# A scan step in two VectorE operations instead of three, gate products in pairs, and a new order of the first stage

## The chip, the cores and the metric

The kernel runs on one core of a Trainium2 chip. The metric is the time of one execution on the device in microseconds; runs are compared by their median. Five engines take part: TensorE (PE in the profile, its weight loads PEld), VectorE (DVE), ScalarE (ACT), GpSimd (POOL) and the queue that issues all transfers (SP).

## The reference, cut to what matters

Three blocks follow each other. The first is an attention with a complex state: 4 batches and 8 heads, 768 positions, head dimension 48. The second is a gated layer (384 to 1536 to 384), the third another one (384 to 2048 to 384), both on 3072 tokens.

```
for t in range(S):
    new_re = ar * S_re - ai * S_im          # ar, ai of position t, |a| held under 0.999
    new_im = ar * S_im + ai * S_re
    S_re, S_im = new_re + outer(k[t], v[t]), new_im
    y[t] = q[t] @ S_re
x = rms_norm(y) * rms_g
u = silu(x @ w_gate) * (x @ w_val)          # 384 -> 1536, "gate product"
h = (u @ w_out) @ w_in2
out = (h * clip(h + 3, 0, 6) / 6) @ w_out2
```

## The kernel before, in words

The recurrence is done in chunks. Seven units of positions (`UNITS`, line 21), the first and the last of 32 positions per chunk, the five between of 64, with two chunks (`c`) side by side in the partitions. In a unit the products of the factors `a` are formed by a scan over half a chunk: `step` (line 443) multiplies the running complex product in `P` by the next factor. It is written three times per position: one product `m4` of 2x2x48 elements (line 449: imaginary and real factor times real and imaginary product), one sum for the new imaginary half (line 451), one difference for the new real half (line 452). `LAt` holds the normalised factors of one unit in two planes, imaginary then real; `steps_norm` (f1 to f8, line 378) makes them, f7 the imaginary plane and f8 the real one. There are 16 such positions in the first and in the last unit and 32 in each of the others, 192 in all.

After the scan of unit n its factors give scaled keys and queries (`sq`, `k1`, `k2`, `x2`, `x1`), which TensorE transposes (`tr`), multiplies into scores (`scores`), chunk sums (`sums`) and outputs (`outs`). `emit_F` (line 554) makes the factors that carry the state from chunk to chunk, of 16 elements per operation, once for each group `g` of batches. `state` updates the carried state, `flip` transposes the normalised output into `x`. Keys, swapped halves of the state and gate products travel through DRAM (`kwrite`, `kload`, `swap`, `u_dr`).

The gated layer follows per half unit of 256 tokens (`steps_M`, line 748). For each of 12 column groups j (`J1`) there are six `gemm` steps: w = 0 the gate and w = 1 the value, three parts of the inner dimension each, and each `gemm` is three matmuls (`mm3`, lines 744 to 746) because a number is kept as a high and a low part. Gate and value of one j share a tile of PSUM, `pm`, 2 x 256 columns; four such tiles rotate. `silu(j)` then applies Silu on ACT to the gate half (line 766), multiplies by the value half on DVE (line 768) and, at odd j, sends both into `u_dr`.

The first stage has its order written out by hand. `ORDER` (line 34) names, two characters each, which step goes on by one part next, and each engine gets its instructions in exactly that order; a part that must wait holds everything behind it on its engine. `ON_POOL` lists the steps whose products (`ttx`, line 364) run on GpSimd instead of VectorE: 16 of them. Behind the written order come the last unit's gated layer and the later layers (line 996 on), which the change leaves as they are except that `silu` is shared.

Of the kernel before, what the change touches and what calls it, by code (L numbers as in the profile page):

```python
# [9 lines left out]
F32 = mybir.dt.float32  # L10
# [8 lines left out]
XW = 112  # L19
IM = 64  # L20
# [26 lines left out]
    "90837z837A84afa290ah7z7Ea97Cag84a97E85857Cai86aj7F91ar7Ban7Faqar7Barao8-aoarak86aoal7P8-am87ap87as88as888989ap938a7Qas7Qapawas93ax7Rayataz7SaAaB7XaD7TaEaFaC7VaG"
    "7UaHaJaIaKaLaCaJ7WaM8aaN8baJaO8baPanaR8c8daS8danaT8eaU8eaV8caWaYaZaQ8fa+aX8faQa-aXb0b1b28g8gaXb3b4b2b58hb68c8hb78ib88iba8jbb8jbc8kbd8wbebfb9bh8xbibgb9bjbkbnbgbl"
    "8xb9bmbobnbpbq8ybnbrbQaubQ8kau8m8zbQbu8l8mbT8naubs8AdlbtbvbwdkbxaubybubB8BbzbAav8nbC8l8FbD8obE8obR8pbIbR8pbF8qbGbRbH8qbJ8rbK8r8lbL8sbM8sbN8tbObBdC8tccdD8udEbPbB"
    "dF8vbIdG8CdH8DdJdK8vdL8DdM8HdN8EbWdIbS8GdPdObWdQdRbPdSdIdPbPdT8vdUbSbSdPdVdXbSdY8IdZ8Jd+d-8Je0e28Ke3e48Me58LdWe6e7e18NbScde9bSbZbSdWeadsebece8edceeebZbXefdob+bX"  # L50
    "doegehb+bUeidobYbVc0cee1e8ejdseke1elendseoepefeqbYercfesefc0eudmcfdoc1dnb-c1dpcgb-evdqchc2dsdremetc2c3cjewdtduemeAc3c4etc5etc4duexeyc5duezeBeCcickeDeEdueFeGeIcu"
    "eJcueKeHcvdvcveOdvcwcwcxcxdvcyeLcyeMczeNdveAc9eHc6eOc9czeHdwclePc6eQc8cAdycAc8dycBcBcCcCdAcDdyc7cDcbcEc7dycbeReSeWcEeVdzeWcacFcFeYcaeWeZeXeZeXdxeZeTeUeXclf2eZf3"
    "cGf4cGf5cHf6cHf7dxdBcIcme+f8cIe+cmcJcJcnf9e+faeVcKfbfce+dBctfdeVfecofge-fhffcqfifjcrfkflcpfnfocLfpcKf8csfqfmfffmfrftfsfff0ftcLf0gpcMcMftcNcNgmf0hTcOfucOfvgmfwf0"
    "hSfxgmfyfAcPfzf1cPfBcQfCfDcQfEcRfFcRfHfGcSfIcSfJcUcTfKcUfLcVfMcVfOfNcWfPcWfHfQcXfOcKfRfScTfTfAgncXcYfUfHfWcTcYd2fXfYgncZfZcZf+c+f-c+g1fVd3g2g3g4g0fVg5g7d8gng6fV"
    "g0g8c-d3g9gagKgbc-gcd0gdd4gfd1ggghgegigjglg7gkgei8dbd9i9d5d1iaibd9icg7ddgodaidd6d1ifigihiiijikglimded7iniogodfglipiedfiqilieirilitdgiuiviliwdcdhixiydiiAiBisiCiz"
    "djgogLiDgoiEiFiHgogoiIiJiKgohWiGiLisiNiMiziGgxiziNgsgMgxiNiOiPgsh+gqiQiRgriSiTgMiVhWiWiXiYh+iZi+hWgtj0h+gthUgNhWhVgwgviUgNj1hXgwiUgOhYgvgPi-guhZgyh+gugyj2gQj3gz"
    "j6i0gzj4h-i0gRgSgAi0j5j7h0j8gAgBi0gCh0h1i1gCh1h2i1h2h3h3i1j9h4jah4jbjdh5jci1gBjejfjgi-h5i2gHh6i-h6gDh7gHh7i4gDh8i4h8h9h9gJhai6i4hagEgJhbgTjhgEjigGjkhbhcgFi4gGj6"
    "gFjjjdjlhcjmjdjvi5gIjvgIjsjsjnjojvjpjri3jshdgTi3juhdhejvjtjqhei7hfjthfgUjwhgjwjtgUjkjAhgjrjBi7jwjrjCjDjEjFjHgVhgjIjJgWjKg-jLjwjMjOgZjPgXjQjGjRjSjxjGgYjTjNjVjUjW"
# [12 lines left out]
ON_POOL = {34, 132, 138, 171, 570, 814, 840, 862, 1104, 1140, 1146, 1150, 1388, 1396, 1614, 1715}
# [164 lines left out]
def attn_moe(tc, io, dbg=None):  # L236
# [64 lines left out]
    LAt = ap.tile([128, 2 * 32 * D], F32, name="LAt", tag="LAt")  # L301
# [40 lines left out]
    def lav(u):  # L342
        n = UNITS[u][0] // 2 * D
        return LAt[:, 0:2 * n].rearrange("p (x n) -> p x n", x=2)

    def steps_load(u):
        C, _ = UNITS[u]
        n = C // 2 * D
        o = _acol(u)

        def f():
            if C == 64 and UNITS[u - 1][0] == 32:
                nc.gpsimd.memset(P[:, 17:33, D:IM], 0.0)
                nc.gpsimd.memset(X2[:, 16:32, D:IM], 0.0)
            yield
            nc.sync.dma_start(lav(u), io["a_all"][:, o:o + 2 * n].rearrange("p (x n) -> p x n", x=2))
        return [(("aload",), f)]
# [20 lines left out]
    def steps_norm(u):  # L378
# [7 lines left out]
        for sp in range(NS):  # L386
# [34 lines left out]
            out += [((f.__name__, sp), f) for f in (f1, f2, f3, f4, f6, f7, f8)]  # L421
# [3 lines left out]
    def steps_scan(u):  # L425
# [17 lines left out]
        def step(j):  # L443
# [677 lines left out]
```

## Time and profile before

| | |
|---|---|
| runs shown | 1234.21, 1244.21, 1246.96 us; median 1244.21 |
| profiled execution | 1235.19 us, its span 1233.4 us |
| TensorE / VectorE / ScalarE / GpSimd busy | 1085.3 / 802.6 / 563.1 / 97.2 us |
| matmuls / VectorE / ScalarE instructions | 10264 / 1808 / 982 |
| granted TensorE clock, mean | 0.974 |
| table loads of ScalarE before Silu / before Ln and Exp | 21 / 21 |

How to read it: the engines run side by side, so each busy time is a share of the same span. The written order ends at 641 us; from there on TensorE is busy 578.9 of 592.4 us. In the busy digits of the page TensorE stands at 0 in the first slice of 31 us and first reaches 9 in the seventh, while VectorE is at 5 to 9 in each of the first 25 slices. A row `a <- b` in a view of waits says what engine and line a sat idle for until b was done.

### The profile page before, as it was taken

To read this page: it belongs to the slowest core of one execution; us is meant where nothing else is said; L and a number is where in the kernel's file an instruction comes from. 1 tells how busy PE (TensorE), PEld (TensorE's weight loads), DVE (VectorE), ACT (ScalarE), POOL (GpSimd) and SP (SyncE) were. 2 spreads that over 40 slices of the span, in tenths; PEclk is the share of its full clock that TensorE was granted. 3 is DMA by queue.
4 is the path that set the end of the run, shared out by engine and by line. 5 is a ranking of instruction groups with operands and counts; after the bars stand their busy time and mean duration, and the time that the engine had idled before them with its cause. 6 is when DMAs were issued, how large, how long until landed. Compare 5 with 4: busy or idle time off the path is not lost.

```text
span 1233.4 us, 24988 instructions
## 1 busy us (share of the span) xinstructions
PE 1085.3 (88%) x10264; PEld 940.2 (76%) x10264; DVE 802.6 (65%) x1808; ACT 563.1 (46%) x982; POOL 97.2 (8%) x115
## 2 busy tenths in 40 slices
PE   0176579999899998988889999899999999999997
PEld 0165479888898888888788888688888888888886
DVE  5979989989879888787669888443333333333332
ACT  5568556456566565644333444233333333333332
POOL 3010001000011001002013222000000000000000
PEclk9999768999999999999999999999999999999999
DMA  8222342642744625635546654220120120110000
GB/s 339 90 77 65 132 116 84 216 107 87 211 100 119 206 69 153 171 90 150 138 137 202 204 148 123 9 86 1 45 69 16 51 69 9 52 35 1 26 1 29
DMA packets 77981, 124.31 MB, mean 101 GB/s; under 512 B 31841, under 2 KB 50402, under 8 KB 77218
## 3 DMA queue, kind: packets, MB, share of 16 engines
q1 hardware_dynamic: 77858, 122.63, 34.3%
q8 instruction: 82, 1.34, 0.5%
q14 instruction: 41, 0.34, 0.1%
HBM read 80.33 MB, written 34.60 MB: 93 GB/s over the span
## 4 chain that ended last, share of the span: by engine, by line
PE 55%; DVE 7%; DMA 4%; ACT 2%; issue 2%; SPq 0%; POOL 0%; DVEq 0%; ACTq 0%
PE po L745 9%; PE po L746 9%; PE po L744 9%; PE ph L744 5%; PE ph L746 5%; PE ph L745 5%; PE pm L744 4%; PE pm L746 3%; PE pm L745 3%; DMA u_dr<-sg 2%; ACT sg L766 1%; DMA JS<-Sst 1%; PE psT L606 1%; PE psY L696 1%; DMA ok_dr<-okc 1%
## 5 line engine op out<-in xcount | busy, mean ns | idle before, releaser
L744 PE MATMUL pm<-xh,wg 128*128 128x256 f32 x864 | 257.5, 299 | 40.4 <-ACT sg L766 26.4
L745 PE MATMUL pm<-xl,wg 128*128 128x256 f32 x864 | 245.0, 284 | 1.4 <-DVE xl L728 1.4
L746 PE MATMUL pm<-xh,wg 128*128 128x256 f32 x864 | 244.6, 283 | 0.7 <-DVE wg L365 0.7
L744 PEld LDWEIGHTS pm<-xh,wg 128*128 128x128 f32 x864 | 165.7, 192 | 55.5 <-ACT sg L766 36.6
L745 PEld LDWEIGHTS pm<-xl,wg 128*128 128x128 f32 x864 | 166.5, 193 | 2.1 <-DVE xl L728 2.0
L746 PEld LDWEIGHTS pm<-xh,wg 128*128 128x128 f32 x864 | 166.5, 193 | 0.9 <-DVE wg L365 0.9
L959 DVE SCALAR_TENSOR_TENSOR r<-r,ph 128x512 f32<-128x512 f32 x96 | 65.8, 685 | 105.4 <-ACT r L958 105.4
L961 DVE TENSOR_TENSOR gl<-r,gh 128x512 fp32r<-128x512 f32 x96 | 68.0, 708 | 94.2 <-ACT gh L960 93.8
L958 ACT ACTIVATE r<-ph,biasz 128x512 f32<-128x512 f32 x96 | 65.8, 687 | 116.3 <-PE ph L746 116.2
L745 PE MATMUL po<-gl,w_h 128*128 128x512 f32 x288 | 114.6, 398 | 3.9 <-DVE gl L961 3.9
L746 PE MATMUL po<-gh,w_l 128*128 128x512 f32 x288 | 114.4, 397 | 0.0
L744 PE MATMUL po<-gh,w_h 128*128 128x512 f32 x288 | 114.1, 396 | 0.0
L746 PE MATMUL ph<-x2b,wi_l 128*128 128x512 f32 x288 | 113.5, 394 | 0.0
L745 PE MATMUL ph<-x2b,wi_h 128*128 128x512 f32 x288 | 113.3, 393 | 0.0
L744 PE MATMUL ph<-x2b,wi_h 128*128 128x512 f32 x288 | 113.1, 395 | 0.0
L960 ACT ACTIVATE gh<-r 128x512 fp32r<-128x512 f32 x96 | 60.6, 632 | 107.1 <-PE po L746 83.0
L766 ACT ACTIVATE sg<-pm 128x256 f32<-128x256 f32 x144 | 53.1, 383 | 112.7 <-PE pm L746 86.2
L915 DVE TENSOR_TENSOR ul<-uu,uh 128x512 fp32r<-128x512 f32 x72 | 50.7, 706 | 75.2 <-ACT uh L914 75.1
L745 PE MATMUL po<-ul,wo 128*128 128x512 f32 x216 | 85.1, 394 | 1.3 <-DVE ul L915 1.3
L914 ACT ACTIVATE uh<-uu 128x512 fp32r<-128x512 f32 x72 | 45.2, 629 | 89.2 <-PE po L746 83.6
L744 PE MATMUL po<-uh,wo 128*128 128x512 f32 x216 | 85.0, 394 | 0.5 <-ACT uh L914 0.5
L746 PE MATMUL po<-uh,wo 128*128 128x512 f32 x216 | 84.7, 392 | 0.0
(148 smaller groups left out, 2060.7 us busy)
## 6 DMA issues: line engine op xcount, KB each, us to landing
u_dr<-sg SPq DMA_DIRECT2D x72, 256.0 KB, 2.9
uu<-u_dr SPq DMA_DIRECT2D x72, 256.0 KB, 2.7
raw<-in_wo_dram SPq DMA_DIRECT2D x28, 384.0 KB, 3.6
wraw<-in_wgv_dram SPq DMA_DIRECT2D x12, 768.0 KB, 13.3
S<-in_s_all_dram SPq DMA_DIRECT2D x24, 384.0 KB, 4.0
K<-k_dr SPq DMA_DIRECT2D x40, 224.0 KB, 4.6
LAt<-in_a_all_dram SPq DMA_DIRECT2D x5, 1536.0 KB, 6.7
JS<-Sst SPq DMA_DIRECT2D x52, 144.0 KB, 4.0
```

The costliest lines, as they stand in the source:

```text
L606: nc.tensor.transpose(ps[:XW, i * 64:(i + 1) * 64], src, ident[g * 64:(g + 1) * 64, g * 64:(g + 1) * 64])
L696: nc.tensor.matmul(psY[c * C:(c + 1) * C, hpar, hp * D:(hp + 1) * D], lhsT=col(b, 1, hpar, c, hp), rhs=Ws[c][:, b % 2, hpar, hp], start=Fa ...
L744: nc.tensor.matmul(ps, lhsT=wh, rhs=xh, start=first, stop=False)
L745: nc.tensor.matmul(ps, lhsT=wh, rhs=xl, start=False, stop=False)
L746: nc.tensor.matmul(ps, lhsT=wl, rhs=xh, start=False, stop=last)
L766: nc.scalar.activation(sg[:, j % 2], hold[j][:, 0], AF.Silu)
L914: nc.scalar.activation(uh, uu, AF.Copy)
L915: (nc.gpsimd if n < 0 else nc.vector).tensor_tensor(out=ul, in0=uu, in1=uh.bitcast(F32), op=ALU.subtract)
L958: nc.scalar.activation(r, ph, AF.Relu, bias=biasz[:, 2:3], scale=sixth)
L959: stt(out=r, in0=r, scalar=1.0, in1=ph, op0=ALU.min, op1=ALU.mult)
L960: nc.scalar.activation(gh, r, AF.Copy)
L961: tt(out=gl, in0=r, in1=gh.bitcast(F32), op=ALU.subtract)
```

## The change

Four things are changed at once, all but one in the first stage.

1. **The scan step.** `LAt` gets a third plane, the imaginary factor negated, made by one more ScalarE operation per normalised part (f9, twelve in all). With the planes im, re, -im, the product `m4` is laid out so that both halves of the new value are sums: one addition of 2 x 48 elements, written to the imaginary half and then, 64 columns below, to the real half, takes the place of the sum and the difference.
2. **Gate products in pairs.** `pm` now holds two column groups j, 2 x 2 x 256 columns, and two such tiles rotate instead of four of half the size. Silu and the product run once for the pair, at odd j, on 512 elements.
3. **Factor products over both groups.** `emit_F` makes its four products once over both `g` (32 elements) instead of once for each; the sums stay per group.
4. **Order.** `ORDER` and `ON_POOL` (25 steps) are new. A buffer size of the compiler for transfers whose descriptors software writes is set to 1024, which makes room for the larger `LAt`.

```diff
-ON_POOL = {34, 132, 138, 171, 570, 814, 840, ...}
+ON_POOL = {124, 258, 285, 376, 549, 551, 561, 656, ...}
...
-    LAt = ap.tile([128, 2 * 32 * D], F32, name="LAt", tag="LAt")
+    LAt = ap.tile([128, 3 * 32 * D], F32, name="LAt", tag="LAt")
...
+            def f9(sl=sl):
+                nc.scalar.activation(LA[:, 2, sl], LA[:, 0, sl], AF.Copy, scale=-1.0)
+            out += [((f.__name__, sp), f) for f in (f1, f2, f3, f4, f6, f7, f9, f8)]
...
-            la = bass.AP(la.tensor, la.offset, [list(la.ap[0]), [HC * D, 2], [0, 2], [1, D]])
+            la = bass.AP(la.tensor, la.offset, [list(la.ap[0]), [HC * D, 2], [HC * D, 2], [1, D]])
             tt(out=m4, in0=la, in1=pj, op=ALU.mult)
             yield
-            tt(out=P[:, j, IM:XW], in0=m4[:, 0, 0], in1=m4[:, 1, 1], op=ALU.add)
-            tt(out=P[:, j, 0:D], in0=m4[:, 1, 0], in1=m4[:, 0, 1], op=ALU.subtract)
+            pn = P[:, j, IM:IM + 1]
+            pn = bass.AP(pn.tensor, pn.offset, [list(pn.ap[0]), [-IM, 2], [1, D]])
+            tt(out=pn, in0=m4[:, :, 0], in1=m4[:, :, 1], op=ALU.add)
...
+            for n, (f, m) in enumerate(((0, 0), (1, 1), (1, 0), (0, 1))):
+                tt(out=Tx[:, n], in0=F[f], in1=M[m], op=ALU.mult)
+            yield
             for g in range(2):
-                tt(out=tr, in0=f0, in1=m0, op=ALU.mult)
-                tt(out=x0, in0=f1, in1=m1, op=ALU.mult)
-                tt(out=tm, in0=f1, in1=m0, op=ALU.mult)
-                tt(out=x1, in0=f0, in1=m1, op=ALU.mult)
-                tt(out=tr, in0=tr, in1=x0, op=ALU.add)
-                tt(out=tm, in0=tm, in1=x1, op=ALU.subtract)
+                tt(out=to(Tr)[:, g], in0=px[:, 0, g], in1=px[:, 1, g], op=ALU.add)
+                tt(out=to(Ti)[:, g], in0=px[:, 2, g], in1=px[:, 3, g], op=ALU.subtract)
...
-            if w == 0 and k == 0:
-                hold[j] = psM.tile([128, 2, 256], F32, name="pm", tag="m", bufs=4)
+            if j % 2 == 0 and w == 0 and k == 0:
+                hold[j // 2] = psM.tile([128, 2, 2, 256], F32, name="pm", tag="m", bufs=2)
...
-            nc.scalar.activation(sg[:, j % 2], hold[j][:, 0], AF.Silu)
+            nc.scalar.activation(sg, pm[:, :, 0], AF.Silu)
             yield
-            tt(out=sg[:, j % 2], in0=sg[:, j % 2], in1=hold[j][:, 1], op=ALU.mult)
+            tt(out=sg, in0=sg, in1=pm[:, :, 1], op=ALU.mult)
...
-    nc = _bacc.Bacc("TRN2", target_bir_lowering=False, num_devices=1)
+    nc = _bacc.Bacc("TRN2", target_bir_lowering=False, num_devices=1, dynamic_dma_scratch_size=1024)
```

## Rows read from the trace of the kernel before

**Rows 1.** Busy time by stretch: us, then busy (count) of each engine, TensorE clock.

```profile
0.00:47.00 47.00, 0.00 (x0) 0.00 (x0) 31.00 (x79) 25.62 (x42) 9.48 (x11) 1.00 0.66 248
47.00:162.00 115.00, 69.52 (x917) 62.63 (x917) 99.08 (x246) 73.85 (x133) 9.54 (x12) 0.91 0.32 98
162.00:198.00 36.00, 29.67 (x609) 27.06 (x608) 29.95 (x68) 17.86 (x33) 1.50 (x4) 0.61 0.39 89
198.00:641.00 443.00, 407.20 (x6144) 378.64 (x6143) 372.33 (x979) 239.46 (x436) 43.02 (x56) 0.99 0.49 138
641.00:1233.40 592.40, 578.91 (x2601) 471.84 (x2599) 270.23 (x439) 206.32 (x340) 33.70 (x32) 1.00 0.22 63
```

**Rows 2.** Timeline of PE where unit 1's first gate matmul starts: start, us, engine, line.

```profile
197.77 0.39 PE L744 MATMUL pm<-xh,wg 128*128 128x256 f32 x1
```

**Rows 3.** Waits of PE between 198 and 641: us in total, times, longest.

```profile
PE pm L744 <- ACT sg L766: 25.0, 43, 2.7
```

**Rows 4.** Timeline around one such wait, idle time before and its releaser in brackets.

```profile
221.74 0.28 PE L745 MATMUL pm<-xl,wg 128*128 128x256 f32 x1
221.85 0.28 PE L746 MATMUL pm<-xh,wg 128*128 128x256 f32 x1
...
222.16 0.38 ACT L766 ACTIVATE sg<-pm 128x256 f32<-128x256 f32 x1 [2.40 <-PE pm L746]
...
222.60 0.38 PE L744 MATMUL pm<-xh,wg 128*128 128x256 f32 x1 [0.47 <-ACT sg L766]
```

**Rows 5.** Longest wait of DVE between 198 and 641.

```profile
DVE sg L768 <- PE pm L746: 16.9, 15, 2.8
```

**Rows 6.** Timeline of DVE: one scan step and the next one's start.

```profile
32.59 0.36 DVE L449 TENSOR_TENSOR m<-LAt,P 128x192 f32<-128x192 f32 x1
32.98 0.21 DVE L451 TENSOR_TENSOR P<-m 128x48 f32<-128x48 f32 x1
33.11 0.20 DVE L452 TENSOR_TENSOR P<-m 128x48 f32<-128x48 f32 x1
33.35 0.36 DVE L449 TENSOR_TENSOR m<-LAt,P 128x192 f32<-128x192 f32 x1
```

**Rows 7.** Groups by line and shape: count, busy us, mean ns, idle before and releasers.

```profile
L451 DVE TENSOR_TENSOR P<-m 128x48 f32<-128x48 f32 x192 | 41.8, 218 | 6.6
L580 DVE TENSOR_TENSOR Ti<-FTq,psF 112x16 f32<-112x16 f32 x14 | 2.3, 161 | 0.0
L768 DVE TENSOR_TENSOR sg<-sg,pm 128x256 f32<-128x256 f32 x144 | 56.4, 414 | 32.6 <-PE pm L746 18.6 <-ACT sg L766 11.6 <-issue 1.1
L929 DVE TENSOR_TENSOR x2b<-po,x2b 128x512 fp32r<-128x512 f32 x18 | 12.4, 688 | 9.1 <-ACT x2b L928 9.0
L395 ACT ACTIVATE T<-LAt 128x768 f32<-128x768 f32 x12 | 10.0, 835 | 8.4 <-DVE LAt L365 6.7 <-DVE LAt L417 1.7
L766 ACT ACTIVATE sg<-pm 128x256 f32<-128x256 f32 x144 | 53.1, 383 | 112.7 <-PE pm L746 86.2 <-DMA u_dr<-sg 25.6
L976 ACT ACTIVATE ob<-po 128x512 f32<-128x512 f32 x12 | 7.2, 598 | 18.2 <-PE po L746 15.9 <-DVE ob L974 2.2
```

**Rows 8.** Timeline of POOL and DVE while a moved product runs on POOL.

```profile
131.64 1.80 POOL L365 TENSOR_TENSOR X<-X 128x768 f32<-128x768 f32 x1 [26.54 <-ACT X L475]
131.68 1.82 DVE L451 TENSOR_TENSOR P<-m 128x48 f32<-128x48 f32 x1
```

**Rows 9.** Timeline around the longest wait of PE behind Silu.

```profile
324.84 0.66 ACT L766 ACTIVATE sg<-pm 128x256 f32<-128x256 f32 x2 [5.30 <-DMA u_dr<-sg]
...
325.55 0.38 PE L744 MATMUL pm<-xh,wg 128*128 128x256 f32 x1 [2.69 <-ACT sg L766]
```

**Rows 10.** Busy time and clock of the stretch right behind that wait.

```profile
326.50:330.00 3.50, 3.50 (x20) 3.50 (x19) 2.88 (x18) 3.43 (x5) 0.00 (x0) 0.52 0.25 80
```

**Rows 11.** Transfer queues of the page: packets, MB, share.

```profile
q1 hardware_dynamic: 77858, 122.63, 34.3%
```

**Rows 12.** Timeline of PE at its longest wait for a gate product.

```profile
141.12 0.58 PE L744 MATMUL pm<-xh,wg 128*128 128x256 f32 x1 [12.02 <-DVE sg L768]
```

More of the change, by code (lines that the diff above doesn't have):

```diff
@@ new lines @@
+    "2z1d0X1d2z1e2K1e2A2A0X2A0X1b1b2A0X1c1a2K1n2B0X2K2D2D1z1z1A2H1A1c2D1B0X1o2C2D2C1B0Y2G2E1C0Y2J2H1C1p1D2K1p1D1E2L4m1E1F2L1F1G0Y2L1G0Y1H1H2L2G2I2H0Y1q1I1I1J1J1K0Y2M"
+    "1q2P1K0Z2I2N2P2S2N1r4l2N0Z1y2I2P2N0Z2O0Z1L1L2Q1M1M1s0Z1N1N1w1O1O1t0Z2Q1P2Q4D1u1v4E1P4F4G1x1Q4H0+1P4I4J1Q4K1R4L1R0+4M4N4O1S0+4Q4R4P4S1S0+274T4U4V1T284W4X0+4Y1T1U"
+    "4Z284+4-1U1V1V0+501W1W1X1X1Z0-1Y1Z1+1+0-1-1-2020210-21220-2223232424253b0-292R262+1Y4P2g512a502+262b522Z4P501Y53542i55262c562R2d572e582j595a2Z2k5b2e5c5e2k5f2f5g"
@@ new lines @@
+    "5d2V2l5h2V2h5i5j2m2-2n2-5k5l5m2o2R5n2R3c2Y2R2R2R304p2Y2X304p2X4p2W2W5o0-5p2T5q312U1031324t5d5r5q5s5t5d105u5v5q3d5w5x4n4t4p4o3d5y5z4q4t5A4r104t334s5B5C103e5E5F5G"
+    "324u3e4v104v355H4v5I335J4v35343f37344w10374w3g5D363h4w384w365D5K3i5L3a4x3j5D385M3v4z3v3k3w4z3w3x4B3x3y393y3a3z395N3l5R4z3z4y5R3A4z5R5Q4y5O5P3A3B4C4A3B3C5U5S5Q5T"
+    "5S4C5Q5S5Z3C5U3l5+5-5U6061625U63643D655V3D5V3E3E3m693F3F3m66673G3G3n5V686a6b3H5V6c6d693u6e3H6f6g5W693I3I6h3J3o6i6j6k6m3J3K6l6n3s3K3L3p6o6p3r6q6r3q6s3L6t6u3t3M6v"
@@ new lines @@
+    "6w6x3M3N6z3N6m6y6A3O7b3L3O5X6m3P3P5X3Q3Q7e7b3R436B6C5X8K446D6E8J7b6F6G5X6H6I6z446J5Y6K6z456L6N6M6O7c6M6P4c6Q7c3R476R466S6T6U6M3S6V6W3S6X6Z486Y3T3T3V6+6-3V3U3W70"
+    "3W3X713X723Y733Y743Z753Z763+7c77787a3+3-793-3U7m7l407m40417z7h7l426Z8-7a7d42907h6Z7d7d917a924e933U94957d967d977d4249984a994f9a4a9c9d4g9e4b9f9b9g4g9h9i4h9j7i4d4i"
+    "7i9k9o4j9l9m9n9o4k7A7n7d8N9b9p9q9r9o9s8R7n9b9t9u9v9w7B9x9y8R9z9A7f8N9B9C9D9E8N7g9F9G7B9B9H9I8R9B9J9K9L9M9N9P7C9Q7C8L9R7D9S8M8N7k7j9O7E7k8P7j8O7F7H7I7o8Q9T8R9U9V"
@@ new lines @@
+    "9W7G9X9Y9O7J8S7o9O7T8T9-7p8T7J7p7q8T7r8T9Z9+7T7q7ra08U7U7U8U7V7K7V8U7s7W7K7t7W7Xa17X7sa27Y7ta37Y8U7v7w9-7v7Z8Va49-7Z7+7u7L7w8X7u7+8X7-7S7-8Z80807y818X7M7x7y7xa5"
+    "818Xadad8W7Q82828Y83a683a784a8adaga98Waaaeaeabaeaf84857Nalamac85867O8+7P86aganao877Rapaq8888agarasat89au89avacaxaw8aay8aazac8bagaAaBaC8b8caD8cah8d8dah8e8e8f8faE"
+    "aFah8h8+ah8gaGaxaHaIaK87aJaiaLax8haj8i8iaj8jbC8j878kbz8k8gd5aMaN8l8laOd68raPajaQaR8gaKajaSaTbzak8saUaKaV8maW8mbA8naYaZ8saXa+8nbAa-8ob08tb1bXb2b3b48ob58pb88Ab6aX"
@@ new lines @@
+    "b78q8ub9ba8x8qaXbb8C8ybcbdbeb8bfbg8y8qbzb8bhbibj8zbkbm8DbAbnbobp8Eblbqbr8Ebs8Fbt8Bbubv8Gblbwbybxdnbldo8Hdpdqdrdsby8Idt8vbYdubydvdw8wdxdydAdBbZdCdzdDdEdFdzdGdHdz"
+    "bZdIdJdKdLbDbBbKbBbBbEb+dNdObKdPb+dQdRbBdSbBdTbBb-dUdVdWc0dMd7c1dZdXc3c4dYd8dMd+d-e0e1bBd9dZc2dMe2e3dZc5e4e5e6e7d9e8e9d9ebecc5edd9eeefddegdabJddbGddbJdbbGcfbMdd"
+    "bHdcbMehc6bHbIbFdfbIdebFdfc6bLdfc7eiejbLbNdfcebNbOeac8enbPcfdgcgbPccdgeacbbOeadgekelemcgeodgepenbQdhchbSchencic9bQeqerbSdjcicjcacddjcjckckclesdjcletcmdleudjbTcm"
@@ L70 @@
+    "pMqeoHp+pIpNoHpIpOp-qfpWpXqeq0qfqfqeqeq0qfpWpXqepPq0pQpWpXpRq0pSpTpVpUq1q2q3q2pVq3q2q3pV"
 )
-ON_POOL = {34, 132, 138, 171, 570, 814, 840, 862, 1104, 1140, 1146, 1150, 1388, 1396, 1614, 1715}
+ON_POOL = {124, 258, 285, 376, 549, 551, 561, 656, 779, 799, 808, 827, 829, 831, 841, 936, 1103, 1107, 1109, 1111, 1113, 1125, 1356, 1360, 1372}
 def _tok0(u):
@@ L567, in emit_F @@
                 continue
-            F = [(FTp, FTq)[c][:, w].rearrange("p g q (b h) -> p g q b h", b=2) for w in range(2)]
-            M = [FT[:, w, :, 0, :, c] for w in range(2)]
+            F = [(FTp, FTq)[c][:, w] for w in range(2)]
+            M = [FT[:, w, :, 0, :, c].rearrange("p g q b h -> p g q (b h)") for w in range(2)]
             Tr = at.tile([XW, 2, 2, 2, 4], F32, name="Tr", tag=f"Tr{c}")
             Ti = at.tile([XW, 2, 2, 2, 4], F32, name="Ti", tag=f"Ti{c}")
-            Tx = at.tile([XW, 2, 2, 2, 2, 4], F32, name="Tx", tag="Tx")
+            Tx = at.tile([XW, 4, 2, 2, 8], F32, name="Tx", tag="Tx")
             to = lambda t: t.rearrange("p g b a h -> p g a b h")
+            for n, (f, m) in enumerate(((0, 0), (1, 1), (1, 0), (0, 1))):
+                tt(out=Tx[:, n], in0=F[f], in1=M[m], op=ALU.mult)
+            yield
+            px = Tx.rearrange("p n g a (b h) -> p n g a b h", b=2)
             for g in range(2):
-                tr, tm = to(Tr)[:, g], to(Ti)[:, g]
-                x0, x1 = Tx[:, 0, g], Tx[:, 1, g]
-                f0, f1, m0, m1 = F[0][:, g], F[1][:, g], M[0][:, g], M[1][:, g]
-                tt(out=tr, in0=f0, in1=m0, op=ALU.mult)
-                tt(out=x0, in0=f1, in1=m1, op=ALU.mult)
-                tt(out=tm, in0=f1, in1=m0, op=ALU.mult)
-                tt(out=x1, in0=f0, in1=m1, op=ALU.mult)
-                tt(out=tr, in0=tr, in1=x0, op=ALU.add)
-                tt(out=tm, in0=tm, in1=x1, op=ALU.subtract)
-                yield
+                tt(out=to(Tr)[:, g], in0=px[:, 0, g], in1=px[:, 1, g], op=ALU.add)
+                tt(out=to(Ti)[:, g], in0=px[:, 2, g], in1=px[:, 3, g], op=ALU.subtract)
+            yield
             res.append((Tr, Ti))
@@ L754, in gemm @@
         def gemm(j, w, k):
-            if w == 0 and k == 0:
-                hold[j] = psM.tile([128, 2, 256], F32, name="pm", tag="m", bufs=4)
+            if j % 2 == 0 and w == 0 and k == 0:
+                hold[j // 2] = psM.tile([128, 2, 2, 256], F32, name="pm", tag="m", bufs=2)
             wh, wl = wgv(j)
             xh, xl = st["x", h]
-            mm3(hold[j][:, w], wh[:, k, w], wl[:, k, w], xh[:, k], xl[:, k], k == 0, k == KT - 1)
+            mm3(hold[j // 2][:, j % 2, w], wh[:, k, w], wl[:, k, w], xh[:, k], xl[:, k], k == 0, k == KT - 1)
         def silu(j):
-            if j % 2 == 0:
-                hold["sg", j // 2] = mo.tile([128, 2, 256], F32, name="sg", tag="sg")
-            sg = hold["sg", j // 2]
+            pm = hold[j // 2]
+            sg = mo.tile([128, 2, 256], F32, name="sg", tag="sg")
             table(None)
-            nc.scalar.activation(sg[:, j % 2], hold[j][:, 0], AF.Silu)
+            nc.scalar.activation(sg, pm[:, :, 0], AF.Silu)
             yield
-            tt(out=sg[:, j % 2], in0=sg[:, j % 2], in1=hold[j][:, 1], op=ALU.mult)
-            if j % 2:
-                yield
-                nc.sync.dma_start(u_dr[j - 1:j + 1, :, t0:t0 + 256].rearrange("j p t -> p j t"), sg)
+            tt(out=sg, in0=sg, in1=pm[:, :, 1], op=ALU.mult)
+            yield
+            nc.sync.dma_start(u_dr[j - 1:j + 1, :, t0:t0 + 256].rearrange("j p t -> p j t"), sg)
         for j in range(J1):
@@ L775, in steps_M @@
                     out.append((("gemm", h, j, w, k), lambda j=j, w=w, k=k: gemm(j, w, k)))
-            out.append((("silu", h, j), lambda j=j: silu(j)))
+            if j % 2:
+                out.append((("silu", h, j), lambda j=j: silu(j)))
         return out
```

57 lines of the change are left out of this document (19 added, 38 removed).

## The prediction

> **What bounds the kernel now.** I read the busy time by stretch first and cut it where the work changes hands [rows 1]. From 641 us on TensorE is busy 578.9 of 592.4 us and nothing there is edited but the pairing of the last unit's Silu, so the change can act only ahead of 641. That part falls in two. Up to 198 us, where unit 1's gated layer begins [rows 2], TensorE has little to do (69.5 of 115, then 29.7 of 36) and VectorE is near full (99.1 of 115, 29.9 of 36): start-up is VectorE's. From 198 to 641 TensorE is busy 407.2 of 443 us and VectorE 372.3. Here the waits decide. Of TensorE's 35.8 idle us, 25.0 go in 43 waits for Silu [rows 3], and VectorE's own longest wait is for TensorE [rows 5]. So the middle is TensorE's, and it can give back 35.8 us at the very most.
>
> The Silu waits need a close look [rows 4]. Silu starts only when the last issued matmul on `pm` has ended; the next matmul starts 0.07 us after Silu's 0.38, a hole of 0.47. That matmul isn't a later column group that lacks a buffer: counted along the matmuls, it is the remainder of the same group's value half. The written order lets Silu of j go ahead of the last one to three `gemm` parts of j at 62 of 132 places, 59 of them in units 1 to 5, and then PE must wait for ACT to leave the tile. The 43 waits are three quarters of these 59.
>
> **The change, part by part.**
>
> *Scan step.* Alone on VectorE a step takes 0.76 us from product to product: 0.39 to the sum, 0.13 to the difference, 0.24 to the next product [rows 6]. One addition of 96 elements replaces the last two stretches (0.37 together). It lasts longer than the 0.21 of 48 elements and less than the 0.36 of 192; interpolated, 0.26, plus the 0.03 by which a dependent successor follows: 0.29. A step saves about 0.08 us, 192 steps 15 us. Bounds: nothing, should the addition take the 0.36 of 192 elements; 0.13 if it is as quick as 48. The Trainium skill, "VectorE: DVE Perf Modes", section on the DRAIN, says that the next operation does not start until the pipe is empty, so that every dropped operation saves its whole duration. By that the saving would be 0.22 + 0.20 - 0.26 = 0.16 a step, 31 us in all. The trace disagrees: the difference starts 0.13 after a sum that lasts 0.21 [rows 6], so I keep 0.08.
>
> *f9* adds twelve ScalarE operations of 768 elements at 0.84 = 10 us [rows 7]. ScalarE is busy 239 of 443 us, and pairing gives 12 us back there. On the path only start-up counts: f9 waits for f7 and the first step for f9, while VectorE does f8, about as long; 0 to 1.7 us for units 0 and 1, taken as 0.
>
> *Pairs.* Silu: 144 x 0.383 becomes 72 x 0.60 (a 512-wide read of PSUM, row of line 976), 55 to 43 us. Product: 144 x 0.41 becomes 72 x 0.69 (row of line 929), 60 to 50 us [rows 7]. Both lie beside TensorE's work. Decoded, the new order has Silu ahead of its own pair's last matmuls at 37 of 66 places, 36 of them in units 1 to 5; three quarters of these, 27, now cost 0.60 + 0.09 = 0.69 each: 18.6 us against 43 x 0.47 = 20. So fewer, longer holes: -1.6. The 25.0 also hold a few that were long because Silu itself waited for the transfer of an older `sg` (2.69 us at 325.5) [rows 9]: about 4.8 us above 0.47 each. A pair's Silu comes a whole column group later behind that transfer, so I take 4 of these away. After such a hole the clock stood at 0.52 for 3.5 us [rows 10]; two fewer are worth up to 3 us, kept for the range.
>
> *Factor products.* Twelve operations of 16 elements become eight in each of 13 places; a dropped one is worth at most 0.16 [rows 7], some 0.09 where it overlaps: 5 us, 1 of them in start-up.
>
> *Order.* What is queued on VectorE ahead of unit 1's first gate matmul, counted in both orders at the rows' pitches: the 48 steps of units 0 and 1 (-3.8); unit 2's steps, 13.5 at 0.76 before, 7.5 at 0.68 now (-5.1), merely put behind it; factor and gate products (-1.3); three `k1` products back from GpSimd (+2.1); one sum to it (-0.6); one masked score more (+0.7). Together -8.0. GpSimd's products also hold VectorE: a sum of 0.21 took 1.82 while one ran [rows 8]. That very product returns to VectorE, another 1.6 us. **Start-up: about -10** (0 if transfers and handovers set it after all, -17 with the larger step saving and no such holds). Past it, 25 steps run on GpSimd instead of 16; with up to 1.6 us each, nine more take 14 us at most from VectorE, which has 70.7 idle us there and loses some 25 of work by the edits.
>
> *Moved transfers.* Key loads, swaps and gate writes keep their number and sizes on SP and change places by a few steps. All 77,858 packets ran on the hardware queue [rows 11], which the smaller buffer for software-made descriptors doesn't concern: nothing. Table loads of ScalarE, counted in both orders, stay at 21 and 21.
>
> **Sum.** Start-up -10; in the middle -1.6 and -4 at Silu, and -1.5 of the other 10.8 us of TensorE's waits because VectorE is earlier: -7. Together -17 on the profiled execution's 1235.2: 1218. That execution was 9 us below the median of the runs shown, 1244.2; -17 on the median gives 1227. I forecast 1222, between them, with 1210 to 1234 as this case's own range.
>
> **Rivals.**
>
> 1. *VectorE sets the middle too.* For it: laid end to end, VectorE's durations make some 88 us for a unit, and a unit takes 88.6 (443 / 5). The stage would then shrink with VectorE's work (about -43 in the middle), until TensorE's 407.2 stop it at -36. With the start-up 1235 - 46 = 1189, more likely 1195 to 1205 since some Silu holes stay. Against: rows 3 and 5, where TensorE waits for Silu and hardly for VectorE. 0.13.
>
> 2. *The gain is absorbed.* TensorE's total ahead of unit 1's gate is the same in both orders and unit 0's matmuls now stretch further towards it; if that order leaves as much idle later, or the longer Silu holes hit at all 36 places (25 us instead of 18.6) while one halved-clock stretch more falls in the middle, 1232 to 1244. Likewise if the 96-wide addition is no cheaper than two. 0.23.
>
> 3. *Slower: two buffers instead of four.* In a plain run of gate matmuls (0.11 us each [rows 4]) a buffer came round after three other groups, 54 matmuls or 6 us; with pairs after one other pair, 36 matmuls or 4 us. A product later than that on VectorE stops TensorE. It has happened: 12.0 us at 141 [rows 12]. If half the 60 pairs of the middle miss by 1 us, that is +30, and 1248 at the profiled execution's level; it decides from an average of 0.3 us a pair on. Against: between 198 and 641 the waits by far most often end with Silu, and VectorE has less queued between matmul and product in the new order. 0.09.
>
> The forecast keeps 0.55.
>
> **From cases to numbers.** About 1% (12 us) is what a measurement of this kernel can tell from no change. Faster by more than that: nearly all of the first case (0.51 of 0.55) and rival 1, 0.64. Slower: rival 3, 0.09. Within 1%: rival 2 and the rest, 0.27. For 8 in 10 the range runs from 1199, leaving out the lower half of rival 1, to 1240, leaving out rival 3 and the upper part of rival 2.
>
> **What would show it.** Right: the new addition at 0.24 to 0.28 us, 192 times; a step in 0.67 to 0.69; unit 1's first gate matmul at 186 to 190 instead of 197.8; about 27 Silu waits near 0.69; the rest from the last gate matmul of the order on as long as before (592 us); the order's end near 624. Wrong: a first gate matmul still at 197 (start-up was not VectorE's); TensorE's busy share of the middle still 92% with other names in its waits (rival 2); long waits on line 768's successor (rival 3); a middle under 420 us (rival 1).

## The result, and the profile after

Four runs of the changed kernel gave a median of 1211.56 us (1208.83 to 1213.81), the kernel before beside them 1244.95 (1234.21 to 1246.96): a ratio of 0.974 with a 95% interval of 0.968 to 0.980. Ratios, here and below, leave out executions over 1.5% above the fastest of the same kernel; medians keep them. The forecast was 1222. The profiled execution took 1209.66 us with a span of 1207.5, 25.9 less span than before. Busy time by stretch, cut at unit 1's first gate matmul (180.0 us) and where the written order and the last unit's gated layer end (609.7, in the table 610, and 640.3), columns as in [rows 1]:

```profile
0.00:47.00 47.00, 0.71 (x3) 0.35 (x4) 30.34 (x67) 26.01 (x43) 9.48 (x11) 1.00 0.66 249
47.00:162.00 115.00, 72.44 (x1123) 64.33 (x1126) 103.35 (x206) 77.21 (x134) 8.08 (x10) 0.93 0.40 114
162.00:180.00 18.00, 16.61 (x406) 14.70 (x405) 16.24 (x29) 14.96 (x30) 4.08 (x5) 1.00 0.26 58
180.00:610.00 430.00, 400.08 (x6155) 374.85 (x6150) 361.15 (x752) 237.94 (x384) 58.06 (x66) 1.00 0.50 142
610.00:640.30 30.30, 29.22 (x220) 28.59 (x219) 21.48 (x38) 8.68 (x17) 8.15 (x8) 0.89 0.62 182
640.30:1207.50 567.20, 554.26 (x2376) 447.37 (x2375) 247.65 (x394) 197.13 (x317) 26.51 (x25) 0.99 0.20 56
```

Against [rows 1] and the marks of before (197.8, 641.2, then 25.8 and 566.4 us): start-up 17.8 us shorter, the middle 443.4 to 429.7, the last unit's gated layer 25.8 to 30.6, the rest 0.8 longer.

The timelines of the changed kernel answer to [rows 2, 4, 6]: the first gate matmul; a scan step and the next one's start, pitch 0.68; one hole behind a Silu.

```profile
180.04 0.39 PE L744 MATMUL pm<-xh,wg 128*128 128x256 f32 x1
...
30.03 0.36 DVE L451 TENSOR_TENSOR m<-LAt,P 128x192 f32<-128x192 f32 x1
30.42 0.26 DVE L455 TENSOR_TENSOR P<-m 128x96 f32<-128x96 f32 x1
30.71 0.36 DVE L451 TENSOR_TENSOR m<-LAt,P 128x192 f32<-128x192 f32 x1
...
382.76 0.28 PE L746 MATMUL pm<-xh,wg 128*128 128x256 f32 x1
383.07 0.60 ACT L765 ACTIVATE sg<-pm 128x512 f32<-128x512 f32 x1 [0.92 <-PE pm L746]
383.72 0.39 PE L744 MATMUL pm<-xh,wg 128*128 128x256 f32 x1 [0.69 <-ACT sg L765]
```

Groups by line and shape in it, for [rows 7]: the addition, the product and the Silu of pairs, f9.

```profile
L455 DVE TENSOR_TENSOR P<-m 128x96 f32<-128x96 f32 x192 | 52.6, 274 | 9.3 <-PE psT L606 1.5
L767 DVE TENSOR_TENSOR sg<-sg,pm 128x512 f32<-128x512 f32 x72 | 48.8, 681 | 29.4 <-ACT sg L765 16.8 <-issue 6.3 <-PE pm L746 3.8
L765 ACT ACTIVATE sg<-pm 128x512 f32<-128x512 f32 x72 | 42.6, 597 | 76.4 <-PE pm L746 70.7 <-DMA u_dr<-sg 5.3
L421 ACT ACTIVATE LAt<-LAt 128x768 f32<-128x768 f32 x12 | 10.1, 838 | 5.3 <-DVE LAt L415 5.3
```

TensorE's waits in its middle, 182 to 610 us, for [rows 3]:

```profile
PE pm L744 <- ACT sg L765: 20.6, 25, 2.5
PE pm L744 <- DVE sg L767: 4.6, 6, 1.9
PE psU L676 <- DVE Sst L646: 1.9, 2, 1.0
PE pm L745 <- DVE xl L728: 1.6, 2, 1.5
```

### The profile page after: what moved, and what is told of

Same layout as the page of the kernel before. It is cut to its first block, busy times and chain, and to the rows that moved or that the text cites. A ratio compares the mean times of both kernels' runs of the same rounds, so it can differ in the third digit from the quotient of the medians.

```text
span 1207.5 us, 24626 instructions
## 1 busy us (share of the span) xinstructions
PE 1073.3 (89%) x10264; PEld 930.2 (77%) x10264; DVE 780.2 (65%) x1483; ACT 561.9 (47%) x922; POOL 114.4 (9%) x124
## 4 chain that ended last, share of the span: by engine, by line
PE 55%; DVE 6%; DMA 3%; ACT 1%; issue 1%; SPq 0%; DVEq 0%; ACTq 0%
PE po L745 9%; PE po L746 9%; PE po L744 9%; PE ph L744 5%; PE ph L745 5%; PE ph L746 5%; PE pm L744 3%; PE pm L745 3%; PE pm L746 3%; PE psT L606 1%; DVE m L451 1%; DMA ok_dr<-okc 1%; DVE P L455 1%; PE psY L696 1%; DMA V<-in_v_dram 1%
## 5 line engine op out<-in xcount | busy, mean ns | idle before, releaser
L744 PE MATMUL pm<-xh,wg 128*128 128x256 f32 x864 | 256.7, 297 | 30.0 <-ACT sg L765 20.6
L765 ACT ACTIVATE sg<-pm 128x512 f32<-128x512 f32 x72 | 42.6, 597 | 76.4 <-PE pm L746 70.7
```

Of the source, the lines that this page charges most:

```text
L744: nc.tensor.matmul(ps, lhsT=wh, rhs=xh, start=first, stop=False)
L765: nc.scalar.activation(sg, pm[:, :, 0], AF.Silu)
```

## The experiments

Three batches, each on one chip beside the kernel before; ratios are to that. "Idle" is TensorE's idle time between unit 1's first gate matmul and the order's end (before 35.8 us, after 29.9), "middle" the time between the two. Views of waits say, as in [rows 3], who waited for whom: us in total, times, longest. Line numbers differ by one to three between kernels. The last column is how much of the middle TensorE stood at a granted clock of 0.50 in the profile (before 10.2 us, after 3.4).

| run | us | ratio, interval | first gate matmul | middle | idle | at 0.50 |
|---|---|---|---|---|---|---|
| old step in after | 1222.92 | 0.984 [0.976, 0.993] | 181.8 | 438.0 | 33.3 | 10.2 |
| order and factors alone | 1218.65 | 0.979 [0.974, 0.983] | 181.8 | 437.5 | 31.7 | 13.7 |
| unpaired, first reading | 1203.56 | 0.970 [0.960, 0.980] | 180.5 | 424.7 | 24.0 | 3.4 |
| unpaired, second | 1207.24 | 0.968 [0.964, 0.973] | 185.1 | 424.4 | 23.2 | 3.4 |
| unpaired, Silu behind | 1204.49 | 0.966 [0.961, 0.970] | 189.0 | 424.1 | 20.2 | 17.1 |
| Silu behind in after | 1219.42 | 0.978 [0.967, 0.988] | 188.1 | 433.8 | 28.5 | 20.5 |
| Silu behind in before | 1227.04 | 0.988 [0.979, 0.996] | 196.3 | 435.3 | 24.1 | 34.1 |
| all on VectorE | 1211.69 | 0.975 [0.966, 0.983] | 188.7 | 428.4 | 27.0 | 6.8 |
| step and f9 in before | 1258.42 | 1.010 [1.001, 1.020] | 198.2 | 467.0 | 42.1 | 54.6 |
| step without f9 in before | 1242.61 | 0.995 [0.991, 0.999] | 195.2 | 450.8 | 35.9 | 27.3 |
| Silu for each group | 1254.96 | 1.010 [1.006, 1.014] | 193.2 | 465.8 | 43.1 | 68.3 |
| wait filled with matmuls | 1214.46 | 0.978 [0.970, 0.987] | 185.7 | 435.0 | 29.5 | 13.7 |

At 0.50 TensorE gets about half as much done (134 matmuls against 256, shown below), so such time costs up to half its length. An estimate from the table: the middle less its idle time and half of the last column is some 402 us before, 398 after, and 389 to 401 in the other runs. The middles thus differ mostly by idle time and clock, and each row has one profile: it can't tell how much of the last column an edit brings about and how much is chance.

**Old step in the kernel after.** The edit:

```diff
-            tt(out=pn, in0=m4[:, :, 0], in1=m4[:, :, 1], op=ALU.add)
+            tt(out=P[:, j, IM:XW], in0=m4[:, 0, 0], in1=m4[:, 1, 1], op=ALU.add)
+            tt(out=P[:, j, 0:D], in0=m4[:, 1, 0], in1=m4[:, 0, 1], op=ALU.subtract)
```

> The changed kernel with the scan step of before (a sum and a difference of 48 elements; the third plane is still made). Theory (start-up is VectorE's, the middle TensorE's): a step 0.76 us instead of 0.68, so unit 1's first gate matmul 4 us later (48 steps x 0.08) than the changed kernel's 180.0, up to 6 with what follows; the middle (429.7 us) longer by 0 to 3. In all +4 to +9: 1216 to 1220 against 1211.6. Rival (VectorE sets the middle as well): 192 x 0.08 = 15 us: 1226. Rival (the step was never on the path, the order alone brought the gain): within 2 of 1212.

11 us slower than the kernel after by the medians, 13 by the ratios, though the two were not run side by side and the intervals overlap. That lies between the two expectations. In the profiles 1.8 us of it are in start-up and 8.3 in the middle: 3.4 of these are idle time, and 6.8 us more at 0.50 cost up to 3.4. The step is worth more than forecast where VectorE was thought not to count.

**Step alone in the kernel before.** The new step and the third plane, with f9 in f7's step:

```diff
+                nc.scalar.activation(LA[:, 2, sl], LA[:, 0, sl], AF.Copy, scale=-1.0)
```

> The kernel before with the scan step in two operations and the third plane, in the order of before, nothing else. Theory: start-up shorter by about 5 us (61 steps queued ahead of unit 1's first gate matmul x 0.08), the middle the same within 2: 1238 to 1241 against 1245. Rival (VectorE sets the middle): -15, 1230. Rival (an order written for three operations has fixed which wait comes last): 1245.

Theory missed: 1.0% slower. ScalarE's and TensorE's waits in its middle:

```profile
ACT LAt L418 <- DVE LAt L417: 20.8, 8, 5.5
...
PE pm L746 <- ACT sg L768: 32.1, 45, 4.5
```

At that place f9 stands at the head of ScalarE's queue up to 5.5 us before VectorE has made its plane, and Silu stands behind it. The middle is 23.6 us longer than in the kernel before, but only 6.3 us of that is idle time; the larger part goes with 54.6 us at 0.50 instead of 10.2.

**Step without f9 in the kernel before.** The edit is the first one turned round. The kernel leaves out the third plane, so the real half is formed as a sum, not as the difference it should be:

> The kernel before, with one change: a scan step's sum and difference become one addition of 2 x 48 elements. No third plane and no f9 is made, so the real half is a sum instead of a difference (its values are wrong, its operations and sizes are those of the kernel after). Theory: the run of the step alone was 1.0% slower only because f9, issued right behind f7, held ScalarE's queue (20.8 us in 8 waits). Without it the shorter step shows: start-up 3 to 4 us shorter, 5 to 12 in all, ratio 0.990 to 0.996. Rival: an order written for the old step loses by the new one itself, through handovers that come at other times: ratio 1.003 to 1.012 as with f9.

In the theory's range by the ratio, 0.995, under it by the medians, which are 3 us apart: the sign is right, the size not settled. In the profile start-up is 2.6 us shorter and the middle 7.4 longer, with as much idle time and 27.3 us at 0.50. Against 1.010 with f9, on another chip, that operation with its plane cost some 19 us there (the intervals leave 6 to 32); 6.2 us of it are idle time in the middle, and the time at 0.50 doubled, 27.3 to 54.6 us. The step itself brings 3 to 6 us in the old order, against 11 in the new.

**Silu behind its own matmuls,** in both kernels. When the order reaches a Silu, the remaining matmuls of its tile are issued first:

```diff
+                if key[1] == "silu" and i not in done:
+                    for jj in (key[3] - 1, key[3]):
+                        for g in of[key[0], key[2], jj]:
+                            if g not in done:
+                                out.append(g)
```

> The changed kernel with one thing moved in its order: the matmuls of a pair that stand behind their own pair's Silu (37 of 66 places) are put right ahead of it, so that TensorE never has to wait for Silu to leave the tile. Theory (the holes are TensorE's time): the 20.6 us of waits for Silu in the middle fall to under 5, the middle from 429.7 to about 414; in all -12 to -18: 1194 to 1200. Rival (the holes only take up slack of a chain that ends on VectorE or ScalarE): other waits fill them, 1208 to 1214. Rival (Silu now starts 0.1 to 0.4 us later and the two buffers are too few): slower, 1215 or more, with waits for the product of line 767.

> The kernel before with the same move: a column group's remaining matmuls go ahead of its own Silu (62 of 132 places). Theory: the 25.0 us of waits for Silu between 198 and 641 fall to about 7 (those behind a transfer stay), the stage ends 12 to 18 earlier: 1227 to 1233 against 1245. Rival (slack): 1242 to 1247.

Right in the kernel before, 19.5 us under it on that chip by the medians and 15 by the ratio; wrong in the kernel after, where a rival came. TensorE's waits, first after, then before, each so edited:

```profile
PE pm L744 <- DVE sg L767: 17.2, 14, 2.5
PE psT L606 <- ACT XTt L612: 2.6, 4, 1.2
...
PE pm L744 <- ACT sg L765: 0.7, 1, 0.7
```

```profile
PE psT L606 <- DVE P L365: 3.9, 1, 3.9
PE pm L744 <- DVE sg L768: 3.5, 5, 1.8
```

The Silu waits went in both (25.0 and 20.6 us). In the kernel before idle time fell by 11.7 us. With pairs it hardly fell (29.9 to 28.5), since 17.2 us of waits for the pair before came instead. That other waits fill the holes is shown; that the kernel is slower than the kernel after is not: the ratios, 0.978 and 0.974, lie within each other's intervals, and its profile has 20.5 us at 0.50 in the middle and a second halved stretch in start-up.

**All products on VectorE.**

```diff
-ON_POOL = {124, 258, 285, 376, 549, ...}
+ON_POOL = set()
```

> The changed kernel with none of its 25 moved products on GpSimd; all run on VectorE in the same order. Before the last unit the 25 products take some 22 us of VectorE; on GpSimd they held VectorE for about 18 us (sum of the excess lengths of VectorE's instructions that ran beside them). Theory (GpSimd takes little off VectorE, because the two-input operations stand still meanwhile): within 4 us of 1211.6. Rival (they are real relief): +10 to +15, 1222 to 1227. Rival (they only do harm, being twice as slow and on the way to the transposes): -5 or more.

As expected, no effect: 0.975 against 0.974, where the intervals leave some 10 us either way. What GpSimd takes from VectorE it gives back in holds, as in [rows 8]; a timeline of the kernel after:

```profile
384.53 2.04 POOL L363 TENSOR_TENSOR P<-S,P 128x768 f32<-128x768 f32 x1 [0.18 <-DMA k_dr<-X]
...
384.88 1.80 DVE L455 TENSOR_TENSOR P<-m 128x96 f32<-128x96 f32 x1
```

The addition that takes 0.26 elsewhere ends 0.11 after GpSimd's product. The Trainium skill, "SBUF — State Buffer", section "Who interferes with whom", says that a VectorE instruction with two inputs in SBUF contends with a GpSimd instruction that reads SBUF, through a shared pair of ports that is locked exclusively; the row agrees.

**Unpaired.** The kernel after with four tiles of one column group each, two Silus and two products of 256 columns at odd j.

```diff
+                hold[j] = psM.tile([128, 2, 256], F32, name="pm", tag="m", bufs=4)
...
+                nc.scalar.activation(sg[:, i], hold[j - 1 + i][:, 0], AF.Silu)
```

> The changed kernel with four tiles of one column group again instead of two of a pair; Silu and product stay where the new order has them, at odd j, but as two operations of 256 each. Theory (pairing only saves fixed time on ScalarE and VectorE): ScalarE +12 us and VectorE up to +10 us in all; a hole behind an early Silu is 0.38 + 0.09 = 0.47 behind the second Silu instead of 0.69, or 0.85 behind both; 1209 to 1217. Rival (the wide operations are what the gain came from): 1222 or more.

> The unpaired kernel once more, for a second reading on this chip beside the three others. If pairing costs what the first reading said, 0.966 to 0.970 of the kernel before, 1201 to 1206; if the first reading was by chance, the level of the kernel after, 0.974 or 1211.

In both readings faster than the kernel after, by 8 and, through the ratios (0.968 to 0.974), by 7 us; the intervals overlap and the two were not run side by side. The profiles say where: idle time is 24.0 and 23.2 us instead of 29.9, with the same 3.4 us at 0.50. Waits of the first reading and one hole:

```profile
PE pm L744 <- ACT sg L765: 14.4, 23, 2.2
PE pm L744 <- DVE sg L768: 4.3, 5, 1.6
...
209.48 0.39 PE L744 MATMUL pm<-xh,wg 128*128 128x256 f32 x1 [0.47 <-ACT sg L765]
```

About as many holes as with pairs, of 0.47 instead of 0.69; waits for products the same (4.3 and 4.6).

**Unpaired, Silu behind.** Both edits together.

> The kernel after with single column groups again (four tiles, Silu and product of 256 columns each, as in the run named unpaired), and every Silu put behind the remaining matmuls of its own two groups (37 of 66 places, as in the run named silu behind). Theory: with pairs this move failed because only one other buffer is left and the waits for Silu (20.6 us) became waits for the product of the pair before (17.2 us). With four tiles the second kind has room (before's own order with the same move: 3.5 us in 5). Then the 14.4 us of Silu waits of the unpaired run go and hardly anything comes: idle time of TensorE in the middle 14 to 18 us instead of 24.0, 1193 to 1199 us. Rival: the order is tight enough that the waits move to another name whatever the number of buffers: 1201 to 1210.

Mostly missed: the Silu waits went, but idle time fell only from 24.0 to 20.2 us, because this came.

```profile
PE pm L744 <- DVE sg L768: 10.4, 11, 2.1
PE psU L676 <- DVE Sst L646: 3.0, 2, 1.6
```

Four tiles soften the exchange (17.2 to 10.4) and don't end it. Its profile has 17.1 us at 0.50 against 3.4, which takes the gain back there. It equals the unpaired kernel within the intervals; these two are the fastest of all.

**Order and factors alone.** Unpaired, with the old step. The third plane and f9 are still made and 25 steps still run on GpSimd, so it is not quite the order and the factor products alone.

> The kernel after with two parts undone: the scan step in three operations again, and single column groups instead of pairs. What is left of the change is the new order and the factor products over both groups. Theory: the step edit is worth about 11 us here too (0.08 x 192 = 15 on VectorE, of which the kernel with pairs showed 11), so 1203 to 1206 of the unpaired run plus 9 to 13: 1212 to 1218; the order is then the largest part of the whole, 27 to 33 us under the kernel before. Rival: without pairs VectorE has slack, and the step is worth under 5: 1203 to 1208.

Expected 1212 to 1218, measured 1218.65: the order with the factor products (and f9) brings 27 us, the step 11 more on the same chip by the medians, 13 by the ratios. TensorE's waits in its middle, and in that of the kernel before the one for gate products:

```profile
PE pm L743 <- ACT sg L764: 13.5, 23, 1.8
PE pm L743 <- DVE sg L767: 8.5, 5, 4.0
PE pm L744 <- DVE xl L727: 2.3, 2, 1.2
PE psX L720 <- DVE xl L727: 2.0, 1, 2.0
```

```profile
PE pm L744 <- DVE sg L768: 0.8, 1, 0.8
```

**Silu for each group.** Unpaired, Silu of the even group right behind its last matmul, its product eight places later.

```diff
+                if key[1] == "gemm" and key[3] % 2 == 0 and key[4:] == (1, KT - 1):
+                    f = first[key[0], key[2], key[3]]
+                    out.append(f)
+                    due.append([f, 8])
```

> The changed kernel with four tiles of one column group, Silu and product of each group on their own (that of even j right behind its last matmul, its product eight order places later), and all of a group's matmuls ahead of its Silu. From the run with only the second move (1219.4, 17.2 us of waits for the product of a pair) and the same move in the kernel before (waits for the product 3.5 us). Theory (with the holes gone the two pair buffers became the limit): waits for Silu and for products in the middle fall to under 8 us together, the middle from 429.7 to 410 to 416; 1195 to 1202. Rival (VectorE's queue decides): 1208 to 1215, with other waits in their place.

Missed by over 50 us; it is 50 us above the unpaired kernel with Silu behind, too. Waits of ScalarE and VectorE, then of TensorE:

```profile
ACT sg L766 <- PE pm L746: 79.4, 44, 6.0
ACT sg L766 <- DMA u_dr<-sg: 41.9, 14, 7.8
...
DVE sg L768 <- ACT sg L766: 39.2, 27, 4.2
```

```profile
PE psT L606 <- ACT XTt L612: 13.6, 10, 2.5
PE psX L721 <- ACT Yt L712: 7.6, 4, 3.2
```

Issued early, Silu waits at the head of ScalarE's queue, and evictions that other work needs stand behind it: f9's mistake again. It waits for its matmuls (79.4 us; unpaired with Silu behind 63.8), and what grew most is its wait for the transfer of an older `sg` (41.9 us in 14 waits there against 7.1 in 4): the edit takes the tile `sg` one group sooner. Of the longer middle 23 us are idle time, and 68.3 us at 0.50 instead of 17.1 cost up to another 26. How the loss divides among the early Silu, the later product and the tile taken sooner is not shown.

**The wait filled with matmuls.** 84 matmuls whose result nothing reads, ahead of unit 1's factors, in a wait of 11 us (119.8 to 131.0). In the kernel after, the clock fell to half within that wait, at 123.1, and stood there until 140.2.

```diff
+                for _ in range(84):
+                    nc.tensor.matmul(ps[:, 0:256], lhsT=wh[:, 0, 0], rhs=xh[:, 0], start=True, stop=True)
```

> The changed kernel with 84 matmuls whose result nothing reads, put into TensorE's longest wait (119.8 to 131.0, ahead of unit 1's factors). Theory (the halved clock from 123 to 140, and the second halved stretch that some runs show behind 155, follow that wait): granted clock 1.00 from 120 to 180; TensorE's 8.3 busy us of 131 to 140 take half; first gate matmul of unit 1 at 174 to 179 instead of 180.0 (or 188.1, as in the run that had the second stretch); runs 1203 to 1209 and closer together. Rival (start-up is VectorE's and the clock costs nothing there): 1209 to 1214. Rival (the added matmuls delay the factors): 1214 or more.

Missed. By stretch, columns as in [rows 1], from the start of the first halved clock on:

```profile
134.60:141.40 6.80, 6.80 (x36) 6.44 (x35) 6.42 (x13) 4.07 (x7) 0.00 (x0) 0.50 0.94 341
141.40:168.70 27.30, 25.53 (x492) 23.24 (x492) 24.03 (x44) 20.12 (x32) 1.47 (x1) 1.00 0.56 135
168.70:182.40 13.70, 13.70 (x158) 12.14 (x155) 8.64 (x19) 8.11 (x18) 3.66 (x5) 0.50 0.15 44
```

The first halved stretch shrank from 17.1 us in the kernel after to 6.8; another came at 168.7 that the profile of after does not have, and the first gate matmul followed at 185.7. The second reading of the unpaired kernel, with the first stretch at its full 17.1 us and the same second one, had it at 185.1: what was saved of the first stretch gained nothing.

## Why the prediction was right and where it was wrong

The forecast, 1222, was 10 us above the median, which lies near the lower end of its range; its sign is right, and so are the sizes of the scan step and of a Silu hole. On the profiled execution -25.9 us came where the sum had -17: 7.8 more in start-up and 6.7 more in the middle, less 5.6 lost behind the order, where it had nothing. That these errors partly cancel is luck. By its own steps:

**Scan step: the size right, the place wrong.** Addition 0.26, step 0.68 against 0.76, as forecast from a difference that started 0.13 after the start of a sum of 0.21 [rows 6]. From the Trainium skill, "VectorE: DVE Perf Modes", section "The DRAIN you can't avoid", the prediction worked out 0.60 and held that the trace disagrees. But that section adds that a next operation which is not held starts earlier, and with that the 0.13 agrees. The 15 us of VectorE's time became 11 us of the whole, not the 3.8 ahead of unit 1's gate that the sum counted: start-up got 1.3 to 1.8 of it (181.8 to 180.0 with pairs, to 180.5 without, in the profiles with no second halved stretch) and the middle 8 to 13. Of the latter, idle time is 3.4 with pairs and 8 without; 3.4 and 5 go with the clock, which may be chance. The step that failed is the one that made the middle TensorE's by the waits of before. They showed VectorE ending few, 6.7 us in all. But the new order moves the balance: with it and the old step, unpaired, 23 Silu holes remain of 43 and waits that VectorE ends rise to 16.7 us, the one for gate products from 0.8 us in the kernel before to 8.5; the new step takes that one to 4.3 and 3.7, and all of them to 8.6 and 6.3. So rival 1 was true in part, in the new order alone, which fits that the step is worth little in the old one.

**Start-up: -10 forecast, -17.8 measured; the clock was left out.** The first gate matmul was forecast at 186 to 190. All four profiles with the old order have two halved stretches between 153 us and that matmul. Of those with the new order five have one and four, the kernel after among them, none (the run with a Silu for each group has a short and a long one). What one costs is seen in the unpaired kernel's two readings, the same instructions, by stretch, first reading and then second (the column behind POOL's is the clock):

```profile
162.00:168.00 6.00, 4.77 (x129) 4.33 (x131) 4.54 (x6) 5.69 (x10) 0.00 (x0) 1.00 0.37 68
168.00:180.00 12.00, 11.44 (x256) 10.00 (x257) 11.12 (x24) 9.02 (x22) 4.49 (x5) 1.00 0.18 50
```

```profile
162.00:168.00 6.00, 5.18 (x148) 4.67 (x141) 5.10 (x6) 5.69 (x10) 0.00 (x0) 1.00 0.30 63
168.00:180.00 12.00, 12.00 (x134) 10.55 (x131) 8.01 (x18) 7.15 (x18) 2.07 (x4) 0.50 0.18 50
```

In 12 us TensorE got 134 matmuls through instead of 256, and unit 1 began at 185.1 instead of 180.5. Where such a stretch lasted 17.1 us, unit 1 began at 188.1, 188.7 and 189.0. So the summed -10 fits the profiles with one stretch, and some 8 us came on top in the profile of after, which has none. The sum counted instructions and left the clock out of this stage. Nor is it shown that the -10 itself is VectorE's queue: the profile of before has two stretches where those have one, and in its second, just ahead of unit 1, TensorE is the fuller engine, 16.12 us of 17.10 against VectorE's 14.07:

```profile
179.70:196.80 17.10, 16.12 (x289) 14.49 (x292) 14.07 (x44) 4.62 (x11) 1.50 (x4) 0.50 0.20 53
```

The step "start-up is VectorE's" was read from a stretch of 36 us that mixes the two. The shorter scan step alone moved unit 1 by 1.3 to 1.8 us in the new order and 2.6 in the old, where a halved stretch was 3.4 us shorter too; 3.8 were counted. Over whole executions the clock rose as well: 0.979 to 0.985 in the four of the changed kernel, 0.955 to 0.977 in the 37 of the kernel before beside the experiments.

**Silu holes: number and price right, the comparison and the transfer term wrong.** 27 holes of 0.69 were forecast: 25 came, 20 of them at 0.69. But the order alone takes 43 holes to 23 or 24; pairs then raise each from 0.47 to 0.69. Setting the old order's 43 x 0.47 against the new one's 27 x 0.69 credited the pairs with the order's work. Pairing costs: 5 to 6 us of Silu waits, 5 of the middle, 4 to 8 of the whole. The 4 us to be had where Silu waits for a transfer failed: waits of 2.22 and 2.48 remain. One, with what Silu had waited for:

```profile
293.31 0.60 ACT L765 ACTIVATE sg<-pm 128x512 f32<-128x512 f32 x1 [4.24 <-DMA u_dr<-sg]
...
293.96 0.58 PE L744 MATMUL pm<-xh,wg 128*128 128x256 f32 x1 [2.22 <-ACT sg L765]
```

**Rival 3, two buffers.** It did not decide: 4.6 us in 6 waits with pairs, 4.3 in 5 without. It would come next: once the Silu holes are taken away, two tiles cost 17.2 us and four 10.4.

**f9 at nothing: it fits, by where it stands.** 5.3 us of ScalarE's idle time over twelve in the new order, and no wait of TensorE with its name; no run leaves it out there. Right behind f7 in the old order, some 19 us.

**GpSimd: right.** Taking its 25 steps back moves the time by nothing that the intervals can tell.

**Middle and tail.** Middle -7 forecast, -13.7 measured: order and factors -5.9 (443.4 to 437.5), step -12.8 (to 424.7), pairs +5.0. Of it, idle time is 5.9; halved stretches fall from 10.2 us to 3.4, worth 3.4; the other 4 I can't give to a row. The last unit's gated layer was forecast as before and lost 4.8: TensorE is busy 29.5 us there against 25.35, with a halved stretch of 6.8 (3.4 lost):

```profile
611.20:618.00 6.80, 6.36 (x28) 6.07 (x29) 0.97 (x3) 1.26 (x2) 1.29 (x1) 0.50 0.57 198
```

The kernels with the new order all have 3.4 or 6.8 us of it in that layer, except the one with a Silu for each group; those with the old order have none. So it goes with the order, though of the change only the pairing reaches that layer, and the unpaired kernels have it too; why is not shown. Together -17.8 - 13.7 + 4.8 + 0.8 = -25.9.

**What stays open.** The factor products were not taken apart from the order, which is thereby the largest part, 27 us, and unexplained in its details. What starts a halved stretch at 168 in one execution and not in another was not found, nor how far those of the middle follow from the edits.

## What to carry to other kernels

Read what bounds a stage from the new schedule, not from the old one: an order that takes one engine's waits away makes the next engine's work count, and an edit worth 3 to 6 us before it was worth 11 after. When two edits fall together, compare each with the kernel that has all the others; a term that improves on the kernel before can still be a loss. An operation that waits in an in-order queue costs what stands behind it: f9 and the early Silu were operations of 0.84 and 0.38 us each, and the edits that placed them so cost some 19 and 50 us. Read the granted clock beside the idle time: as far as one profile each tells, more than half of the first loss and up to half of the second was time at half clock.

## What the runs showed of the hardware

- One execution of the same instructions had TensorE at half clock, 0.50, for 13.7 us in start-up and another not; unit 1 began 4.6 us later in the first. TensorE was busy all of 12.00 us of it and got 134 matmuls done, against 256. Keeping TensorE busy in a wait ahead of another such stretch shortened that one from 17.1 to 6.8 us and gained nothing.
- In this program, a Silu on a tile with matmuls still to come held TensorE for its own length and 0.09 more: 0.38 gave 0.47, 0.60 gave 0.69.
- A product on GpSimd held a two-input VectorE operation until 0.11 us after its end (1.80 us instead of 0.26): 25 steps moved there brought nothing that the intervals can tell.
